# Delta-rule attention with two feed-forward layers on one core: triangles inverted in two halves joined on TensorE, two output products held over a group's end, square root by Newton steps

## The chip, the cores and the metric

One NeuronCore of a Trainium2 chip runs the whole program. TensorE does the matrix products (PE in the profile, its weight loads PEld), VectorE (DVE) and ScalarE (ACT) the elementwise work and the emptying of PSUM, GpSimd (POOL) some elementwise work between tiles of SBUF, and SyncE (SP) issues the DMAs. The metric is the device time of one execution in microseconds; lower is better.

## The reference

```python
B, H, S, D = 4, 8, 768, 48
k_n = k / (np.linalg.norm(k, axis=-1, keepdims=True) + 1e-06)
for t in range(S):                     # one 48x48 state for each of 4 x 8 heads
    y[:, :, t] = q_t @ state
    v_old = state.T @ k_t
    state = state + beta_t * outer(k_t, v_t - v_old)
x = y.transpose(0, 2, 1, 3).reshape(3072, 384)
x = (silu(x @ w_gate) * (x @ w_val)) @ w_out       # d_ff 1536
h = x @ w_in                                       # d_ff 2048
out = where(h > 0, h, exp(min(h, 0)) - 1) @ w_out2
```

## The kernel before, in words

**Groups.** The 3072 tokens are worked in 12 groups of 256: 128 steps of time of 2 of the 4 batches. A group holds 16 units (batch, head) of 128 time steps, and each unit is cut into 4 chunks of 32 steps, one on each 32 partitions. Within a chunk the recurrence is solved in closed form, which needs the inverse of a 32x32 unit triangular matrix: 64 triangles for a group.

**Attention of a group.** `norm` sums the squares of the keys (on GpSimd, into the buffer `ain`), takes the root on ScalarE (L168) and makes the factor 1/(norm + 1e-6) in six small instructions on VectorE (L170 to L175); `nkn` scales the keys (L184), `kb` multiplies by beta, `trans` transposes queries and keys on TensorE (L200), `gram` makes the 32x32 products of keys and of queries with keys (L210), and VectorE masks them into `gr` (L213). `inversion` brings the 64 triangles with `transpose` into a layout in which each partition holds half the columns of a triangle (L227) and solves them in SBUF on VectorE: for each row l from 31 down to 1 a product (L248, `mul`) and a sum (L255, `add`), over 16 - l//2 columns. Where such a step has over `CUT` = 40 elements it is made as two instructions, so that a group has 58 of each kind. `back` transposes the result (L263), and ScalarE copies it in four `spread` steps (L270) into `zt`, where the triangles of two chunks lie as a block diagonal of 64x64. `xstep` multiplies `R` (keys and values) by it with 32 products of 64x64 tiles (L281; the trace counts two instructions for each product of plain 32-bit floats, 64 here). Then come `gstep` (L294; ScalarE and VectorE take its results out of PSUM, L298 and L299), `chain` (the state from chunk to chunk, L312 and L316), `yall` (the outputs, L325), and `xtr` (outputs transposed and split in a high and a low part, `xh` and `xl`).

**First layer.** For each group and each of 12 blocks f of the hidden layer, `gv1` makes gate and value (18 products of 128x128 by 256 columns, L445) in one of two PSUM buffers `gv`. The result goes through ScalarE (Silu, L466), VectorE (L467), ScalarE (high part, L345) and VectorE (low part, L348) into one of `NHB` = 3 buffers `hb`. `out1` (9 products, L479) adds block f to `acc`, always two blocks behind `gv1` (`LAG` = 2); at the end of a group both that are left are made (`while held:` in `moe1`), then ScalarE copies `acc` out (L486) and it is stored to the buffer `x2d` in memory.

**Order.** `attention(g + 1)` and `moe1(g)` are lists of steps with weights, and `merge` sorts both together by the share of the weights that lies ahead of a step. The inversion of group g + 2 stands in the list of attention of group g + 1, its last fifth at the start of the next group (`XTR` = 0.8). From this order Tile sets each engine's own, and may move an instruction ahead where its inputs come early. Each engine works its queue strictly in order.

**Start and end.** Group 0 and the inversion of group 1 run while weights arrive and are decoded (64-bit words to floats, L389 to L409 and L345, L348, temporaries in turn). The second layer begins after group 11: `h2` (L514), the nonlinearity (L518 to L521), `out2` (L531); its weights are decoded through the temporaries `gr`, `st`, `zt`, `dt`.

Of the kernel before, what the change touches and what calls it, by code (L numbers as in the profile page):

```python
# [21 lines left out]
def delta_moe_kernel(ctx: ExitStack, tc: tile.TileContext, q, k, v, beta,  # L22
# [39 lines left out]
    NHB = 3  # L62
# [4 lines left out]
    zd = T("zd", [128, 2, 16])  # L67
# [8 lines left out]
    zt = T("zt", [128, 16, 64])  # L76
    st = T("st", [128, B, DM])
    sv = T("sv", [128, 2, C - 1, DM])
    sm = [T(f"sm{n}", [128, 16]) for n in range(5)]
# [25 lines left out]
    def emit_consts():  # L105
# [8 lines left out]
        fl = sm[0][:, 0:1]  # L114
        V.tensor_reduce(out=fl, in_=ident.rearrange("p (r h m) -> p h r m", r=4, h=2)[:, 1],
                        op=ALU.add, axis=AX.XY)

        V.tensor_copy(zd[:, 1, :], fl.to_broadcast([128, 16]))
        V.tensor_scalar(out=zd[:, 0, :], in0=zd[:, 1, :], scalar1=-1.0, scalar2=1.0,
                        op0=ALU.mult, op1=ALU.add)  # L120

    def emit_zero():
        V.memset(kp[:, :, D:64], 0.0)
        V.memset(qp[:, :, D:64], 0.0)
        G.memset(zt, 0.0)
# [36 lines left out]
    def norm(g):  # L162
        i, b0 = ax_of(g)
        sq = ain[:, 0:768].rearrange("p (u d) -> p u d", d=D)
        ss, s, r, t, w = sm
        (G if g > 0 else V).tensor_tensor(out=sq, in0=kp[:, :, 0:D], in1=kp[:, :, 0:D], op=ALU.mult)
        V.tensor_reduce(out=ss, in_=sq, op=ALU.add, axis=AX.X)
        A.activation(out=s, in_=ss, func=ACTF.Sqrt)  # L168

        V.tensor_scalar(out=r, in0=s, scalar1=1e-18, scalar2=None, op0=ALU.max)  # L170
        V.reciprocal(out=r, in_=r)
        V.tensor_tensor(out=t, in0=ss, in1=r, op=ALU.mult)
        V.tensor_tensor(out=t, in0=t, in1=s, op=ALU.add)
        V.tensor_scalar(out=t, in0=t, scalar1=-0.5, scalar2=-1e-6, op0=ALU.mult, op1=ALU.add)
        V.reciprocal(out=w, in_=t)  # L175
# [5 lines left out]
    def nkn(g, a):  # L181
        u = slice(a * 8, a * 8 + 8)
        kk = kp[:, u, 0:D]
        V.tensor_tensor(out=kk, in0=kk, in1=sm[4][:, u].unsqueeze(2).to_broadcast([128, 8, D]),  # L184
                        op=ALU.mult)
        A.copy(out=R[:, u, 0:D], in_=kk)
# [32 lines left out]
    def inversion():  # L219
        lst = []  # L220
        an = ain.rearrange("p (l j) -> p l j", l=32)

        def start(n):
            def f():
# [3 lines left out]
                if n == 0:  # L228
                    z = buf['z'] = TT("z", [128, 32, 16])
                    G.memset(z, 0.0)  # L230
                    V.tensor_copy(win(z[:, 0:1, 0:1], [[16, 2], [33, 16]]), zd)
# [3 lines left out]
        def step(l):  # L235
            c0 = l // 2
            cuts = [(c0, 16)]
            if l * (16 - c0) > CUT:
                cuts = [(c0, c0 + (16 - c0) // 2), (c0 + (16 - c0) // 2, 16)]

            b = 32 * (l + 1) % 1024
            ts = [ain[:, b + l * (x - c0):b + l * (y - c0)].rearrange("p (j n) -> p j n", n=y - x)
                  for x, y in cuts]

            def mul():
                z = buf['z']
                for (x, y), t in zip(cuts, ts):
                    V.tensor_tensor(out=t, in0=z[:, l:l + 1, x:y].to_broadcast([128, l, y - x]),  # L248
                                    in1=an[:, l, 0:l].unsqueeze(2).to_broadcast([128, l, y - x]),
                                    op=ALU.mult)  # L250

            def add():
                z = buf['z']
                for (x, y), t in zip(cuts, ts):
                    V.tensor_tensor(out=z[:, 0:l, x:y], in0=z[:, 0:l, x:y], in1=t, op=ALU.add)  # L255
            return [mul, add]
        for l in range(31, 0, -1):
            lst += step(l)

        def back():  # L260
            z = buf['z']
            t = ain[:, 0:512]
            V.transpose(out=t.rearrange("p (u i two) -> p i two u", u=16, two=2),  # L263
                        in_=z.rearrange("p a i -> p i a"))
        lst.append(back)

        def spread(r):
            def f():
                q0 = slice(32 * r, 32 * r + 32)
                A.copy(out=zt[q0, :, 32 * (r % 2):32 * (r % 2) + 32],  # L270
                       in_=ain[q0, 0:512].rearrange("p (u i) -> p u i", u=16))
            return f
        return lst + [spread(r) for r in range(4)]


    def xstep():
        for n in range(4):
            p = nxt(atb, "at")[:, 0:384].rearrange("p (n w) -> p n w", n=4)
            for j in range(4):
                for r in (0, 64):  # L280
# [507 lines left out]
```

## Time and profile before

| | |
|---|---|
| median of 3 runs | 1311.82 us (1307.21 to 1316.99) |
| span of the profiled execution, first to last instruction | 1301.1 us |
| median less that span: what lies around it | 10.7 us |
| TensorE busy, mean granted clock | 1162.0 us (89%), 0.949 |
| VectorE, ScalarE, GpSimd busy | 821.8, 608.6, 129.9 us |

The own time of the profiled execution is not among the three, only its span is known, so a change in the span is set against the median. Matmuls overlap in TensorE's pipeline: the time that a block of them takes is the step from its start to the start of the next block, not the sum of their durations. The granted clock is 1.00 at 2.4 GHz and 0.50 at 1.2 GHz; a stretch with a figure between holds some of both.

### The profile page before, as it was taken

How to read it: one execution, taken by the hardware profiler on the slowest of the kernel's cores; microseconds unless marked ns; L12 is line 12 of the kernel's file. 1: busy time of each engine (PE TensorE's matmuls, PEld its weight loads, DVE VectorE, ACT ScalarE, POOL GpSimd, SP SyncE). 2: the span in 40 equal slices, each digit the busy share in tenths (PEclk: the TensorE clock that was granted, in tenths of full speed). 3: DMA queues.
4: the chain of work that ended last, by engine and by line, in shares of the span. 5: the costliest groups of instructions: out<-in, count | busy, mean ns of one | idle time of the engine just before them, and what ended most of it. 6: DMA issues, size and time to landing. Idle time of an engine off the chain costs nothing.

```text
span 1301.1 us, 31342 instructions
## 1 busy us (share of the span) xinstructions
PE 1162.0 (89%) x13086; PEld 1078.5 (83%) x13086; DVE 821.8 (63%) x2709; ACT 608.6 (47%) x1181; POOL 129.9 (10%) x106
## 2 busy tenths in 40 slices
PE   2473999898989898989898989989899999999998
PEld 1363889898888898989888989978689899899897
DVE  6799585848484858585848574467964545454443
ACT  7554534343425252535353524457754545454443
POOL 4353100000000000000000000031300000000000
PEclk9866798889999999999999999989999999999999
DMA  9530202020202020202020100373010101000000
GB/s 298 160 81 1 38 14 39 13 39 10 43 2 51 2 50 2 51 2 50 7 46 2 26 11 5 125 251 104 1 49 1 49 1 49 1 33 1 25 1 25
DMA packets 106815, 57.16 MB, mean 44 GB/s; under 512 B 76945, under 2 KB 101521, under 8 KB 106673
## 3 DMA queue, kind: packets, MB, share of 16 engines
q1 hardware_dynamic: 106672, 55.16, 16.7%
q8 instruction: 102, 1.67, 0.5%
q14 instruction: 41, 0.33, 0.1%
HBM read 45.71 MB, written 9.44 MB: 42 GB/s over the span
## 4 chain that ended last, share of the span: by engine, by line
PE 57%; DVE 34%; ACT 4%; issue 3%; DMA 1%; POOL 1%; SPq 0%; DVEq 0%; ACTq 0%; POOLq 0%
PE gv L445 14%; DVE z L255 7%; DVE ain L248 7%; PE acc L531 7%; PE at L531 7%; PE at L514 7%; PE gv L514 7%; PE acc L479 5%; PE at L294 4%; DVE w L404 2%; PE at L281 2%; DVE hb L348 2%; DVE tb L467 2%; DVE ain L227 2%; PE at L312 2%
## 5 line engine op out<-in xcount | busy, mean ns | idle before, releaser
L445 PE MATMUL gv<-xh,w 128*128 128x256 f32 x1728 | 295.9, 295 | 23.6 <-DVE tb L467 22.9
L445 PEld LDWEIGHTS gv<-xh,w 128*128 128x128 f32 x1728 | 248.9, 200 | 29.4 <-DVE tb L467 24.0
L479 PE MATMUL acc<-hb,w 128*128 128x256 f32 x1296 | 194.9, 298 | 37.6 <-ACT hb L345 34.7
L479 PEld LDWEIGHTS acc<-hb,w 128*128 128x128 f32 x1296 | 172.2, 199 | 45.5 <-ACT hb L345 36.7
L445 PE MATMUL gv<-xl,w 128*128 128x256 f32 x864 | 160.6, 295 | 1.5 <-DVE xl L348 1.5
L466 ACT ACTIVATE tb<-gv 128x256 f32<-128x256 f32 x144 | 54.9, 382 | 216.4 <-PE gv L445 216.0
L467 DVE TENSOR_TENSOR tb<-gv,tb 128x256 f32<-128x256 f32 x144 | 60.7, 422 | 127.6 <-ACT tb L466 126.7
L445 PEld LDWEIGHTS gv<-xl,w 128*128 128x128 f32 x864 | 131.7, 202 | 2.9 <-DVE xl L348 1.7
L345 ACT CAST hb<-tb 128x256 fp32r<-128x256 f32 x144 | 58.4, 406 | 146.8 <-DVE tb L467 146.2
L255 DVE TENSOR_TENSOR z<-z,ain 128x60 f32<-128x60 f32 (+32 forms) x696 | 122.5, 214 | 1.3
L248 DVE TENSOR_TENSOR ain<-z,ain 128x60 f32<-128x60 f32 (+32 forms) x696 | 122.3, 207 | 1.2
L348 DVE TENSOR_TENSOR hb<-tb,hb 128x256 fp32r<-128x256 f32 x144 | 76.7, 533 | 42.7 <-ACT hb L345 41.3
L521 DVE SCALAR_TENSOR_TENSOR hb<-at,hb 128x512 f32<-128x512 f32 x48 | 33.2, 691 | 84.5 <-ACT hb L520 84.5
L521 DVE SCALAR_TENSOR_TENSOR hb<-gv,hb 128x512 f32<-128x512 f32 x48 | 33.1, 690 | 80.2 <-ACT hb L520 72.5
L294 PE MATMUL at<-gr,R 32*96 32x80 f32 x1536 | 75.3, 276 | 8.7 <-DVE w L299 4.4
L294 PEld LDWEIGHTS at<-gr,R 32*96 32x96 f32 x1536 | 64.9, 179 | 19.0 <-DVE w L299 4.6
L520 ACT ACTIVATE hb<-hb,neg 128x512 f32<-128x512 f32 x96 | 69.4, 723 | 2.8
L518 ACT ACTIVATE hb<-at 128x512 f32<-128x512 f32 x48 | 28.6, 595 | 87.6 <-PE at L514 87.6
L518 ACT ACTIVATE hb<-gv 128x512 f32<-128x512 f32 x48 | 28.6, 596 | 85.3 <-PE gv L514 85.0
L281 PE MATMUL at<-R,zt 64*64 64x96 f32 x768 | 38.6, 254 | 27.5 <-ACT zt L270 27.4
L519 ACT ACTIVATE hb<-hb 128x512 f32<-128x512 f32 x96 | 60.6, 632 | 2.7
L281 PEld LDWEIGHTS at<-R,zt 64*64 64x64 f32 x768 | 35.8, 140 | 29.7 <-ACT zt L270 28.2
(174 smaller groups left out, 2154.6 us busy)
## 6 DMA issues: line engine op xcount, KB each, us to landing
w<-in_moe_w_out_dram SPq DMA_DIRECT2D x28, 384.0 KB, 6.6
w<-in_moe_w_in_dram SPq DMA_DIRECT2D x16, 384.0 KB, 5.6
kp<-in_k_dram SPq DMA_DIRECT2D x12, 384.0 KB, 5.4
qp<-in_q_dram SPq DMA_DIRECT2D x12, 384.0 KB, 4.3
w<-in_moe_w_gate_dram SPq DMA_DIRECT2D x12, 384.0 KB, 7.8
w<-in_moe_w_val_dram SPq DMA_DIRECT2D x12, 384.0 KB, 8.0
R<-in_v_dram SPq DMA_DIRECT2D x24, 192.0 KB, 2.6
x2d<-hb SPq DMA_DIRECT2D x12, 256.0 KB, 2.1
```

Of the source, the lines that this page charges most:

```text
L248: V.tensor_tensor(out=t, in0=z[:, l:l + 1, x:y].to_broadcast([128, l, y - x]), in1=an[:, l, 0:l].unsqueeze(2).to_broadcast([128, l, y - x] ...
L255: V.tensor_tensor(out=z[:, 0:l, x:y], in0=z[:, 0:l, x:y], in1=t, op=ALU.add)
L281: nc.tensor.matmul(p[r:r + 64, j], lhsT=zt[r:r + 64, 4 * n + j, :], rhs=R[r:r + 64, 4 * n + j, :], start=True, stop=True, skip_group_check ...
L294: nc.tensor.matmul(ps_[c][0:96, s * 80:s * 80 + 80], lhsT=R[t, u, :], rhs=gr[t, u, 0:80], start=True, stop=True, skip_group_check=True)
L348: (e2 or V).tensor_tensor(out=lo, in0=src, in1=hi.bitcast(F32), op=ALU.subtract)
L445: nc.tensor.matmul(dst, lhsT=wt[:, a_, kk * 128:(kk + 1) * 128], rhs=xx[:, kk, :], start=(n == 0), stop=(n == 3 * KD - 1))
L467: V.tensor_tensor(out=s, in0=p[:, TB:2 * TB], in1=s, op=ALU.mult)
L479: nc.tensor.matmul(o, lhsT=w[:, a_, d * 128:(d + 1) * 128], rhs=hh[:, b_, :], start=(f == 0 and n == 0 and d != 1), stop=(f == F1 - 1 and ...
L514: nc.tensor.matmul(p, lhsT=W[f][:, 0, a_, kk * 128:(kk + 1) * 128], rhs=x2[n][b_][:, kk, :], start=(m == 0), stop=(m == 3 * KD - 1))
L520: A.activation(out=r, in_=r, func=ACTF.Identity, bias=neg1, scale=1.0)
L521: V.scalar_tensor_tensor(out=r, in0=p, scalar=0.0, in1=r, op0=ALU.max, op1=ALU.add)
L531: nc.tensor.matmul(ob4[t], lhsT=hh[:, b_, t * 128:(t + 1) * 128], rhs=w[:, a_, :], start=(f == 0 and m == 0), stop=(f == F2 - 1 and m == 2))
```

## The change

**Inversion.** A triangle is cut into two diagonal blocks of 16x16 and the block below them. VectorE inverts both diagonal blocks in the same instructions, 15 rows instead of 31, and no step is cut in two: 15 products and 15 sums for a group. `back` makes a second transpose, of the whole buffer. `join1` multiplies the block-diagonal inverse by the triangle on TensorE (64 products with 16 rows, 32x32 tiles into one PSUM bank), VectorE adds the unit diagonal and masks (one instruction over 128x512 from PSUM), `join2` multiplies once more on TensorE (64 products), and one copy of 128x512 on ScalarE fills `zt`, in place of the four `spread` copies. `xstep` then has 64 products of 32x32 tiles in place of 32 of 64x64.

**Held products.** Two blocks of `out1` are left over at a group's end and made in the next group; `NHB` is 4.

**Root.** ScalarE's square root and the six instructions are replaced by 13 on VectorE: a first guess from the bits, three Newton steps of three instructions, two more and a reciprocal. `zt` is half as large and no temporary of the decoding any more (`t2`).

```diff
-    NHB = 3
+    NHB = 4
...
-    zd = T("zd", [128, 2, 16])
+    zd = T("zd", [128, 2])
...
-    zt = T("zt", [128, 16, 64])
+    zt = T("zt", [128, 16, 32])
+    eye = T("eye", [128, 32])
+    low = zd[:, 1:2]
...
-        ss, s, r, t, w = sm
+        ss, s, r = sm
         (G if g > 0 else V).tensor_tensor(out=sq, in0=kp[:, :, 0:D], in1=kp[:, :, 0:D], op=ALU.mult)
         V.tensor_reduce(out=ss, in_=sq, op=ALU.add, axis=AX.X)
-        A.activation(out=s, in_=ss, func=ACTF.Sqrt)
-
-        V.tensor_scalar(out=r, in0=s, scalar1=1e-18, scalar2=None, op0=ALU.max)
-        V.reciprocal(out=r, in_=r)
-        V.tensor_tensor(out=t, in0=ss, in1=r, op=ALU.mult)
-        V.tensor_tensor(out=t, in0=t, in1=s, op=ALU.add)
-        V.tensor_scalar(out=t, in0=t, scalar1=-0.5, scalar2=-1e-6, op0=ALU.mult, op1=ALU.add)
-        V.reciprocal(out=w, in_=t)
+        V.tensor_scalar(out=s.bitcast(I32), in0=ss.bitcast(I32), scalar1=-0.5,
+                        scalar2=float(0x5f3759df), op0=ALU.mult, op1=ALU.add)
+        for _ in range(3):
+            V.scalar_tensor_tensor(out=r, in0=s, scalar=-0.5, in1=ss, op0=ALU.mult, op1=ALU.mult)
+            V.tensor_tensor(out=r, in0=r, in1=s, op=ALU.mult)
+            V.scalar_tensor_tensor(out=s, in0=r, scalar=1.5, in1=s, op0=ALU.add, op1=ALU.mult)
+        V.tensor_tensor(out=r, in0=ss, in1=s, op=ALU.mult)
+        V.tensor_scalar(out=r, in0=r, scalar1=-1.0, scalar2=-1e-6, op0=ALU.mult, op1=ALU.add)
+        V.reciprocal(out=s, in_=r)
...
+        d1 = ain[:, 0:512].rearrange("p (u j) -> p u j", u=16)
+        d1t = ain[:, 512:1024].rearrange("p (u j) -> p u j", u=16)
...
         def step(l):
             c0 = l // 2
-            cuts = [(c0, 16)]
-            if l * (16 - c0) > CUT:
-                cuts = [(c0, c0 + (16 - c0) // 2), (c0 + (16 - c0) // 2, 16)]
-
-            b = 32 * (l + 1) % 1024
-            ts = [ain[:, b + l * (x - c0):b + l * (y - c0)].rearrange("p (j n) -> p j n", n=y - x)
-                  for x, y in cuts]
+            n = 8 - c0
+            t = win(ain[:, 512:513], [[8, 2], [32, l], [1, n]])
 
             def mul():
                 z = buf['z']
-                for (x, y), t in zip(cuts, ts):
-                    V.tensor_tensor(out=t, in0=z[:, l:l + 1, x:y].to_broadcast([128, l, y - x]),
-                                    in1=an[:, l, 0:l].unsqueeze(2).to_broadcast([128, l, y - x]),
-                                    op=ALU.mult)
+                V.tensor_tensor(out=t, in0=win(z[:, l:l + 1, c0:c0 + 1], [[264, 2], [0, l], [1, n]]),
+                                in1=win(ain[:, 32 * l:32 * l + 1], [[528, 2], [1, l], [0, n]]),
+                                op=ALU.mult)
 
             def add():
-                z = buf['z']
-                for (x, y), t in zip(cuts, ts):
-                    V.tensor_tensor(out=z[:, 0:l, x:y], in0=z[:, 0:l, x:y], in1=t, op=ALU.add)
+                z = win(buf['z'][:, 0:1, c0:c0 + 1], [[264, 2], [16, l], [1, n]])
+                V.tensor_tensor(out=z, in0=z, in1=t, op=ALU.add)
             return [mul, add]
-        for l in range(31, 0, -1):
+        for l in range(15, 0, -1):
             lst += step(l)
 
         def back():
-            z = buf['z']
-            t = ain[:, 0:512]
-            V.transpose(out=t.rearrange("p (u i two) -> p i two u", u=16, two=2),
-                        in_=z.rearrange("p a i -> p i a"))
-        lst.append(back)
-
-        def spread(r):
-            def f():
-                q0 = slice(32 * r, 32 * r + 32)
-                A.copy(out=zt[q0, :, 32 * (r % 2):32 * (r % 2) + 32],
-                       in_=ain[q0, 0:512].rearrange("p (u i) -> p u i", u=16))
-            return f
-        return lst + [spread(r) for r in range(4)]
+            V.transpose(out=ain[:, 0:512].rearrange("p (u i two) -> p i two u", u=16, two=2),
+                        in_=buf['z'].rearrange("p a i -> p i a"))
+            V.transpose(out=d1t, in_=d1)
+
+        def join1():
+            p = buf['jp'] = nxt(atb, "at").rearrange("p (u j) -> p u j", u=16)
+            for u in range(16):
+                for c in range(C):
+                    r = 32 * c
+                    nc.tensor.matmul(p[r:r + 32, u],
+                                     lhsT=gr[r:r + 16, u, 80:112],
+                                     rhs=d1t[r:r + 16, u], start=True, stop=True,
+                                     skip_group_check=True)
+            v = buf['v'] = TT("z", [128, 16, 32])
+            V.scalar_tensor_tensor(out=v, in0=p, scalar=low[:, 0:1],
+                                   in1=eye.unsqueeze(1).to_broadcast([128, 16, 32]),
+                                   op0=ALU.mult, op1=ALU.add)
+
+        def join2():
+            p = nxt(atb, "at").rearrange("p (u j) -> p u j", u=16)
+            for u in range(16):
+                for c in range(C):
+                    t = slice(32 * c, 32 * c + 32)
+                    nc.tensor.matmul(p[t, u], lhsT=buf['v'][t, u], rhs=d1[t, u], start=True,
+                                     stop=True, skip_group_check=True)
+            A.copy(out=zt, in_=p)
+        return lst + [back, join1, join2]
...
     def xstep():
         for n in range(4):
             p = nxt(atb, "at")[:, 0:384].rearrange("p (n w) -> p n w", n=4)
             for j in range(4):
-                for r in (0, 64):
-                    nc.tensor.matmul(p[r:r + 64, j], lhsT=zt[r:r + 64, 4 * n + j, :],
-                                     rhs=R[r:r + 64, 4 * n + j, :], start=True, stop=True,
+                for c in range(C):
+                    t = slice(32 * c, 32 * c + 32)
+                    nc.tensor.matmul(p[t, j], lhsT=zt[t, 4 * n + j, :],
+                                     rhs=R[t, 4 * n + j, :], start=True, stop=True,
                                      skip_group_check=True)
             A.copy(out=R[:, 4 * n:4 * n + 4, :], in_=p)
...
-        while held:
+        while held and g == NB - 1:
             put(1, held.pop(0), 1.0, out1)
...
-        t2 = ("gr", "st", "zt", "dt")
+        t2 = ("gr", "st", "dt")
```

On TensorE, at the end of a group, the order was this (`w14` and `w17` are the pairs that hold `out1`'s weights, `hb1` and `hb2` with the numbers 280 and 282 belong to the last two blocks, `w0` is the first `gv1` of the next group):

```order
L479 MATMUL acc_85<-hb0_278_7430,w14_53_926 128x256 x9
L479 MATMUL acc_85<-hb1_280_7487,w17_60_1086 128x256 x9
L445 MATMUL gv0_83<-xh1_268_7172,w0_21_203 128x256
L479 MATMUL acc_85<-hb2_282_7542,w17_60_1086 128x256 x9
L445 MATMUL gv0_83<-xh1_268_7172,w0_21_203 128x256 x2
L445 MATMUL gv0_83<-xl1_269_7173,w0_21_203 128x256 x3
```

And this is what stands there now, from the end of the next group's first `gv1` on:

```order
L460 MATMUL gv0_82<-xh1_274_7795,w0_21_210 128x256 x3
L270 MATMUL at1_86<-ain_72,gr_71 32x32 x64
L494 MATMUL acc_84<-hb2_288_8081,w17_61_1096 128x256 x8
L284 MATMUL at2_87<-ain_72,z_293_8221 32x32 x64
L494 MATMUL acc_84<-hb2_288_8081,w17_61_1096 128x256
L460 MATMUL gv1_83<-xh1_274_7795,w1_22_229 128x256 x3
L460 MATMUL gv1_83<-xl1_275_7796,w1_22_229 128x256 x2
L296 MATMUL at3_88<-R_69,zt_73 32x96 x16
L296 MATMUL at0_85<-R_69,zt_73 32x96 x16
L296 MATMUL at1_86<-R_69,zt_73 32x96 x16
```

Before, both products of the end stood in a row with only one instruction between them; now the first gv1 of the next group and `join1` stand ahead of the eleventh block's product, and `join2`, the second gv1, `xstep` and the first `gstep` ahead of the twelfth's.

On ScalarE at the same place, the queue was (`zt<-ain` are the spread copies, `tb1_281` and `hb2_282` the last block's):

```order
L345 CAST hb1_280_7487<-tb0_279_7484 128x256
L270 COPY zt_73<-ain_72 32x16x32 x2
L466 ACTIVATE tb1_281_7539<-gv1_84 128x256
L270 COPY zt_73<-ain_72 32x16x32 x2
L345 CAST hb2_282_7542<-tb1_281_7539 128x256
L486 COPY hb0_283_7572<-acc_85 128x512
L486 COPY hb1_284_7575<-acc_85 128x256
```

Now it is (`tb1_289` and `hb3_290` are the last block's, `tb0_291` and `hb0_292` the next group's first):

```order
L360 CAST hb2_288_8081<-tb0_287_8078 128x256
L481 ACTIVATE tb1_289_8111<-gv1_83 128x256
L360 CAST hb3_290_8114<-tb1_289_8111 128x256
L481 ACTIVATE tb0_291_8148<-gv0_82 128x256
L360 CAST hb0_292_8151<-tb0_291_8148 128x256
L286 COPY zt_73<-at2_87 128x512
L299 COPY R_69<-at3_88 128x384
L299 COPY R_69<-at0_85 128x384
```

The copies into `zt` stood ahead of the last block's Silu and cast; the one copy now stands behind them and behind those of the next group's first block.

On TensorE in group 0, whose queue ran into `xstep` so (`w5` with `hb2` is the third block's product):

```order
L479 MATMUL acc_85<-hb2_66_1152,w5_33_522 128x256 x9
L445 MATMUL gv1_84<-xh0_39_681,w7_35_605 128x256 x3
L445 MATMUL gv1_84<-xl0_40_682,w7_35_605 128x256
L281 MATMUL at1_87<-R_69,zt_73 64x96
L281 MATMUL at2_88<-R_69,zt_73 64x96
L281 MATMUL at3_89<-R_69,zt_73 64x96
L281 MATMUL at0_86<-R_69,zt_73 64x96
```

it now runs:

```order
L460 MATMUL gv1_83<-xh0_40_762,w7_36_686 128x256 x3
L494 MATMUL acc_84<-hb3_70_1430,w5_34_603 128x256 x3
L270 MATMUL at3_88<-ain_72,gr_71 32x32 x64
L494 MATMUL acc_84<-hb3_70_1430,w5_34_603 128x256 x6
L460 MATMUL gv0_82<-xh0_40_762,w9_39_759 128x256 x2
L284 MATMUL at0_85<-ain_72,z_62_1166 32x32 x64
L460 MATMUL gv0_82<-xh0_40_762,w9_39_759 128x256
L460 MATMUL gv0_82<-xl0_41_763,w9_39_759 128x256 x3
L460 MATMUL gv0_82<-xh0_40_762,w9_39_759 128x256 x2
L296 MATMUL at1_86<-R_69,zt_73 32x96 x16
```

The fourth `gv1` and its product now stand whole ahead of `xstep`, and part of the fifth.

## Rows read from the trace of the kernel before

**Rows 1.** The profile page: busy time, share of the span and instructions of each engine.

```profile
PE 1162.0 (89%) x13086; PEld 1078.5 (83%) x13086; DVE 821.8 (63%) x2709; ACT 608.6 (47%) x1181; POOL 129.9 (10%) x106
```

**Rows 2.** The chain of waits of the whole span, one piece: the xstep of group 2.

```profile
192.92 2.79 PE at L281 x64
```

**Rows 3.** The chain of waits in 776 to 906 us, pieces.

```profile
785.38 2.79 PE at L281 x64
...
795.52 2.35 PE gv L445 x18
...
814.01 2.16 PE gv L445 x18
816.17 1.50 PE at L325 x128
```

**Rows 4.** Stretches of a group: length, busy time by engine, granted clock, DMA, GB/s.

```profile
588.70:653.50 64.80, 60.16 (x925) 56.93 (x924) 44.06 (x195) 26.63 (x63) 4.70 (x5) 0.97 0.15 26
...
642.20:646.30 4.10, 0.01 (x1) 0.00 (x0) 1.06 (x3) 3.25 (x6) 1.44 (x2) 1.00 0.00 0
646.30:648.40 2.10, 2.06 (x9) 1.76 (x10) 2.10 (x2) 0.00 (x0) 1.07 (x1) 0.59 0.00 0
648.40:653.50 5.10, 5.10 (x39) 4.97 (x38) 2.24 (x10) 4.03 (x6) 0.00 (x0) 0.83 0.24 80
```

**Rows 5.** PE's instructions in order of time: start, us, line, count, [idle before].

```profile
46.87 6.34 PE L281 MATMUL at<-R,zt 64*64 64x96 f32 x64 [26.95 <-ACT zt L270]
...
127.75 1.01 PE L445 MATMUL gv<-xh,w 128*128 128x256 f32 x3 [11.56 <-DVE tb L467]
...
646.31 2.40 PE L479 MATMUL acc<-hb,w 128*128 128x256 f32 x9 [4.09 <-ACT hb L345]
...
791.52 0.92 PE L294 MATMUL at<-gr,R 32*96 32x80 f32 x32
...
853.88 0.96 PE L514 MATMUL at<-lc,w 128*128 128x512 f32 x3 [2.16 <-ACT w L345]
```

**Rows 6.** ACT's instructions in order of time, at the end of that group.

```profile
642.91 1.25 ACT L270 COPY zt<-ain 32x512 f32<-32x512 f32 x2 [2.41 <-DVE ain L263]
644.18 0.38 ACT L466 ACTIVATE tb<-gv 128x256 f32<-128x256 f32 x1
...
645.85 0.40 ACT L345 CAST hb<-tb 128x256 fp32r<-128x256 f32 x1
```

**Rows 7.** DVE's instructions in order of time: the inversion, then the end of that group.

```profile
619.18 0.19 DVE L248 TENSOR_TENSOR ain<-z,ain 128x31 f32<-128x31 f32 x1
619.41 0.21 DVE L255 TENSOR_TENSOR z<-z,ain 128x31 f32<-128x31 f32 x1
...
641.75 1.07 DVE L263 STREAM_TRANSPOSE ain<-z 128x512 f32<-128x512 f32 x1
...
646.29 1.36 DVE L348 TENSOR_TENSOR hb<-tb,hb 128x256 fp32r<-128x256 f32 x1 [1.26 <-ACT hb L345]
...
651.16 0.17 DVE L170 TENSOR_SCALAR sm<-sm 128x16 f32<-128x16 f32 x1 [2.65 <-ACT sm L168]
```

**Rows 8.** The chain of waits in 588 to 656 us, by line, then pieces.

```profile
by line: PE gv L445 22.5%; DVE z L255 11.2%; DVE ain L248 11.0%; PE at L281 7.7%; PE acc L479 6.9%; PE at L294 6.5%; DVE hb L348 4.3%; DVE tb L467 4.0%; DVE ain L227 3.2%; ACT zt L270 2.8%; PE at L312 2.6%; PE at L200 2.6%; issue 2.3%; DVE 
...
602.22 0.39 ACT tb L466
...
603.53 0.80 DVE hb L348
...
607.98 1.75 PE at L200 x16
```

**Rows 9.** DVE in order of time, second layer: one instruction over 128x512 from PSUM.

```profile
887.20 0.69 DVE L521 SCALAR_TENSOR_TENSOR hb<-gv,hb 128x512 f32<-128x512 f32 x1 [7.71 <-PE at L514]
```

**Rows 10.** All engines in order of time, the squares on POOL.

```profile
645.90 1.47 POOL L166 TENSOR_TENSOR ain<-kp 128x768 f32<-128x768 f32 x1 [1.89 <-ACT zt L270]
```

**Rows 11.** A stretch after group 3's xstep, columns as in rows 4.

```profile
269.60:276.40 6.80, 6.70 (x59) 6.16 (x62) 2.25 (x8) 3.35 (x10) 0.83 (x1) 0.62 0.16 31
```

More of the change, by code (lines that the diff above doesn't have):

```diff
@@ L75, in delta_moe_kernel @@
     ain = T("ain", [128, 1024])
-    zt = T("zt", [128, 16, 64])
+    zt = T("zt", [128, 16, 32])
+    eye = T("eye", [128, 32])
+    low = zd[:, 1:2]
     st = T("st", [128, B, DM])
     sv = T("sv", [128, 2, C - 1, DM])
-    sm = [T(f"sm{n}", [128, 16]) for n in range(5)]
+    sm = [T(f"sm{n}", [128, 16]) for n in range(3)]
     neg1 = T("neg1", [128, 1])
@@ L112, in emit_consts @@
                             pattern=[[1, 32]], channel_multiplier=-1)
-        fl = sm[0][:, 0:1]
-        V.tensor_reduce(out=fl, in_=ident.rearrange("p (r h m) -> p h r m", r=4, h=2)[:, 1],
+        for r in range(4):
+            q0 = slice(32 * r, 32 * r + 32)
+            V.tensor_copy(eye[q0], ident[q0, q0])
+        V.tensor_reduce(out=low, in_=ident.rearrange("p (r h m) -> p h r m", r=4, h=2)[:, 1],
                         op=ALU.add, axis=AX.XY)
-        V.tensor_copy(zd[:, 1, :], fl.to_broadcast([128, 16]))
-        V.tensor_scalar(out=zd[:, 0, :], in0=zd[:, 1, :], scalar1=-1.0, scalar2=1.0,
+        V.tensor_scalar(out=zd[:, 0:1], in0=low, scalar1=-1.0, scalar2=1.0,
                         op0=ALU.mult, op1=ALU.add)
@@ L124, in emit_zero @@
         V.memset(qp[:, :, D:64], 0.0)
-        G.memset(zt, 0.0)
         G.memset(st[0:32], 0.0)
@@ L183, in nkn @@
         kk = kp[:, u, 0:D]
-        V.tensor_tensor(out=kk, in0=kk, in1=sm[4][:, u].unsqueeze(2).to_broadcast([128, 8, D]),
+        V.tensor_tensor(out=kk, in0=kk, in1=sm[1][:, u].unsqueeze(2).to_broadcast([128, 8, D]),
                         op=ALU.mult)
@@ L230, in f @@
                     G.memset(z, 0.0)
-                    V.tensor_copy(win(z[:, 0:1, 0:1], [[16, 2], [33, 16]]), zd)
+                    V.tensor_copy(win(z[:, 0:1, 0:1], [[16, 2], [33, 16]]),
+                                  zd.unsqueeze(2).to_broadcast([128, 2, 16]))
             return f
@@ L632, in delta_moe_kernel @@
     POOL = 0
-    CUT = 40
     LAG = 2
```

## The prediction

> **What bounds the kernel now.** I read the page first, then the chain of waits of one steady group, then TensorE (PE) in order of time where a group ends, with the stretches there. The page puts PE at 89% of the span, DVE at 63% and ACT at 47% [rows 1]: PE is the bound, and the question is where its other 11% lies. The `xstep` of group 2 (counted from 0) starts at 192.92 [rows 2] and that of group 11 at 785.38 [rows 3]: nine intervals of a group in 592.5 us, 65.8 on average, where a steady one takes 64.80 [rows 4]. What is left is a start, in which PE waits 26.95 us for `zt` and once 11.56 us for DVE's `tb` [rows 5], and an end after group 11.
>
> Within a steady group PE stands still in one place of 4.10 us, at the group's end [rows 4], and the idle time is put down to ACT's `hb` [rows 5]. The other group ends look alike. PE's wait names a cast on ACT, but ACT's own rows show what made that late: ACT waited 2.41 us for the transpose of the inversion, copied `zt` at 642.91 and only then came to the last block's Silu (644.18) and cast (645.85) [rows 6]. The transpose began at 641.75 and took 1.07 [rows 7]. So DVE's inversion ends last, and PE pays for it through ACT's queue. The chain of waits agrees: the sums and products of the inversion (L255, L248) are 22.2% of its 68 us [rows 8], 15.1 us, which end in front of that cast.
>
> The stop costs more than its own length. After it the granted clock is 0.59 for 2.10 us and 0.83 for 5.10 us [rows 4]: 2.1 × 0.41 + 5.1 × 0.17 = 1.7 us lost. Without stop and slow clock this group would take 64.8 − 4.1 − 1.7 = **59.0 us**, the floor that I add to.
>
> **The inversion.** Removed on DVE: 58 products and 58 sums; added, 15 and 15. A dependent pair steps by 619.41 − 619.18 = 0.23 us [rows 7], so some 15.1 us of chain become 30 × 0.23 = 6.9, plus a second transpose (1.07, the first's duration) and one instruction from PSUM, for which I take 0.69, a row of the same size from PSUM [rows 9]. DVE then needs 8.7 where it needed 15.1, the transposes are through 5 to 6 us before the group's end, and the wait of 4.1 goes, with its slow clock. That DVE has room again is worth nothing more by itself: PE is next, everywhere else in the group.
>
> Added on PE: two times 64 products, 128 instructions each, in 32x32 tiles. The trace has no such tile. Nearest is `yall` (L325), 128 instructions in 1.50 us [rows 3], 12 ns each; `xstep`, in 64x64 tiles with 96 columns, has 64 in 2.79 us [rows 3], 44 ns each. `trans` gives the price of a column where nothing overlaps: 16 instructions of 128 columns in 1.75 us [rows 8], 0.85 ns a column. So `xstep`'s 64 × 96 columns would be 5.2 us one after the other, and in 2.79 two tiles nearly overlap. With four tiles at a time 128 × 32 columns are 128 × 32 × 0.85 / 4 = 0.9 us, by `yall` 1.5. I take 1.35 for each join (bounds 1.0 and 1.5, leaving a start of the pipeline), nearer to `yall`, since both are many small products: **+2.7**. They stand between products of full size; a `gv1` that is entered from other work stepped 2.35, an undisturbed one 2.16 [rows 3], so each join brings a switch of 0.2: **+0.4**.
>
> `join2` waits for DVE's instruction, and what is queued behind it on PE is the last product of the eleventh block, the second `gv1` and `xstep`. In front of DVE's instruction stands the low part of the next group's first block: Silu to the end of the low part is 602.22 to 603.53 + 0.42, about 1.75 [rows 8] (0.80 in the row is with its waiting), and with 0.69 that is 2.5 us from the end of the first `gv1`. PE has `join1` (1.35) and eight of nine products (0.96) until then, 2.3. I charge **+0.25** (0 to 1; DVE's row at 646.29 took 1.36 beside POOL's work [rows 7, 10]).
>
> The copy into `zt` is one of 128x512 on ACT, some 0.6 us from half of the row of two at 642.91 [rows 6]; in front of `xstep` PE has one product and five of `gv1`, 0.7 us. Nothing, but it has no margin. `xstep` itself has twice the products with half the rows: in four tiles at a time the same 96 columns take the same **2.8** (case C below says otherwise).
>
> **The held products.** No work is added: 18 products move from before the boundary behind it. What they buy is that PE has `gv1` and `join1` to do while the last two blocks go through ACT and DVE, so the chain ACT-DVE-ACT-DVE of the last block no longer ends in front of PE. ACT's queue has the Silu and cast ahead of the copy now, which removes the 4.1 a second time: either part alone might do that. `NHB` = 4 pays for the longer life of `hb`. `acc` is finished later, behind `xstep`, and its copy and store have a group of time.
>
> **The root.** ACT loses a root and the change of table around it, and DVE's wait of 2.65 us for it goes [rows 7]. In its place stand 13 small instructions, at the inversion's step of 0.23 some 3.0 us, where six took 1.4. This lies behind the boundary, in front of DVE's emptying of `gstep` (L314). POOL's squares (1.47 [rows 10]) must wait for `join2`, which reads the same buffer, so `norm` starts a little later than before. The wait of 2.65 and the 13 instructions about cancel; for `gstep` and `chain` coming late I charge **+0.5** (0 to 1.0).
>
> **The clock.** The steady group loses nothing besides the 1.7 above, but the mean interval is 1.0 longer than the steady one, and one place where it goes is 269.60 to 276.40, after the `xstep` of group 3: 6.8 us at 0.62 with PE busy for 6.70 [rows 11], between pieces of `gstep`; 6.8 × 0.38 = 2.6 us. So the clock also falls with no stop ahead of it. The change puts 256 more small instructions there. I charge a loss of **0.85** a group, one such stretch in every third group (0 to 3.4: one in each group, and 0.8 of lesser ones).
>
> The sum of a group: 59.0 + 2.7 + 0.4 + 0.25 + 0.5 + 0.85 = 63.7, against the mean of 65.8: 2.1 less, times nine intervals, **−19 us**.
>
> **Start and end.** In group 0 PE waits for `zt` until 46.87 [rows 5]; the inversion of group 0 is shorter by 6 us, but ACT and the decoding stand in its way, so I take −3 for it. The inversion of group 1 lies in a stretch that DVE bounds (the wait of 11.56 for `tb` at 127.75 [rows 5]): −2 of its 6; and one more `gv1` and `out1` stand ahead of group 0's `xstep` and fill waiting time, 2.2 + 1.3, −3. Together **−8** (0 to −14). At the end `zt` is no temporary of the decoding any more, and the last two products of group 11 remain; PE waited 2.16 there for a decoded weight [rows 5]. I take **−2** (−5 to +3).
>
> Together −29: the span goes from 1301.1 to 1272. The profiled execution's own time isn't known, but the median lies 10.7 above its span; set against the median, 1311.8 − 29 = **1282**.
>
> **Rivals.** B: *the clock falls in every group*, as at 269.60, since `join1`, `join2`, `xstep` and `gstep` now come within some 10 us. Then a group loses 3.4 and not 0.85, 2.55 × 9 = +23: 1305. For it: that stretch lies beside small tiles. Against: the steady group has the same tiles, and its only loss follows a stop.
>
> C: *only two small tiles overlap*, as two do in `xstep` now. Then `xstep` takes 64 × 2 × 96 × 0.85 / 2 = 5.2 in place of 2.8 (+2.4), and each join 1.75 (+0.8 for both): 3.2 × 12 groups = +38: 1320. `yall`, with 12 ns an instruction, speaks against it.
>
> D, the slow side: *products of different row strips into one PSUM bank run one at a time.* Then `xstep` takes 128 × 96 × 0.85 = 10.4 us and each join 3.5: 7.6 + 4.3 = +11.9 over my sum in each of 12 groups, +143: 1425. It decides from the point at which joins and `xstep` together take over 5.5 + 29 / 12 = 7.9 us. For it: `gstep`, whose 32 instructions of 80 columns in four strips took 0.92 [rows 5], 29 ns each and not 68, has a bank for each strip. Against it: two strips of 64 rows went into one bank in `xstep` at 44 ns, not 82 [rows 3]. The Trainium skill, "TensorEngine Tiling (Array Packing)", section "Restrictions and Gotchas", says that different row tiles cannot access the same PSUM bank simultaneously, which is case D; for two strips the trace disagrees (44 ns an instruction), for four no row here shows it.
>
> E, better: no clock loss, joins at 1.0 and no wait at `join2`: 59.0 + 2.0 + 0.4 + 0.25 = 61.65, 2.05 × 9 = −18 more, and the start at its best, −7: 1257.
>
> That nothing happens at all is part of B and C: DVE's chain off the path, and its worth spent on PE.
>
> **Chances.** The forecast 1282 with its own bounds, 1262 to 1298: 0.58; E 0.15; B 0.14; C 0.08; D 0.05. The range takes in E and B, 1256 to 1306. Within 1% is 1298.7 to 1324.9, about what a measurement of this kernel can tell from no change. B and C, less the part of B under that line and with the upper edge of the forecast, give 0.15 there; D and the upper tail of C 0.07; the rest, 0.78, is faster.
>
> **What would show it.** PE without idle time over 1 us at the group ends, and granted clock 1.00 there; DVE's L263 transposes ended before the last block's Silu; the two joins at 1.35 each and `xstep` at 2.8 (over 5 is C, over 10 is D); idle time of PE ahead of `join2` under 0.5; intervals between `xstep` near 63.7; the first `xstep` near 44. The prediction is wrong if the new wait at `join2` or at `chain` is over 2 us, or a stretch under 0.7 of clock stands in each group.

## The result and the profile after

The changed kernel takes **1269.69 us** (median of 4 runs, 1266.85 to 1271.71) against 1309.51 for the kernel before (4 runs, 1300.85 to 1316.99): ratio **0.970, 95% interval 0.965 to 0.976**. The profiled span is 1269.8 us, 31.3 under the 1301.1 of before. The experiments show where it comes from: the held products, with their fourth buffer and without the joined inversion, give more than the whole change, and the joined inversion, once the products are held, costs time.

First the page of the changed kernel (engines, then the DMA queue that carries instructions).

```profile
PE 1178.4 (93%) x16926; PEld 1089.8 (86%) x16926; DVE 733.0 (58%) x1788; ACT 561.9 (44%) x1112; POOL 127.0 (10%) x105
...
q8 instruction: 132, 2.16, 0.7%
```

VectorE is down by 89 us [rows 1] and PE up by 16. `xstep` starts in group 2 at 181.15 and in group 11 at 748.95 (before: 192.85 and 785.31 by PE's own first instruction, 0.07 ahead of the pieces in [rows 2] and [rows 3]), so nine intervals take 567.8 us, 63.1 each. The nine intervals before and after, then two of those of the changed kernel (columns as in [rows 4]):

```profile
192.85:785.31 592.46, 548.97 (x8317) 521.36 (x8317) 396.18 (x1740) 241.21 (x570) 40.69 (x44) 0.96 0.14 25
181.15:748.95 567.80, 553.37 (x11201) 522.25 (x11200) 332.64 (x1045) 203.84 (x515) 41.21 (x45) 1.00 0.12 26
...
368.80:433.50 64.70, 61.69 (x1244) 57.98 (x1243) 37.09 (x116) 22.71 (x57) 4.67 (x6) 1.00 0.12 27
433.50:495.50 62.00, 61.10 (x1243) 57.68 (x1242) 36.83 (x116) 22.59 (x57) 4.65 (x6) 1.00 0.12 28
```

PE's idle time in the nine intervals falls from 43.5 us to 14.4, and its busy time rises by only 4.4, although the joins add more. The granted clock is 1.00 in every interval from group 2 on; before, it was 0.96 over the nine. That difference is worth some 24 us (an estimate, 0.04 of 592.46). PE in order of time at a group's end:

```profile
551.97 1.29 PE L270 MATMUL at<-ain,gr 16*32 16x32 f32 x128
553.18 1.21 PE L494 MATMUL acc<-hb,w 128*128 128x256 f32 x8
554.59 0.45 PE L284 MATMUL at<-ain,z 32*32 32x32 f32 x30 [0.19 <-DVE z L275]
555.63 1.03 PE L284 MATMUL at<-ain,z 32*32 32x32 f32 x98 [0.59 <-issue]
556.58 0.38 PE L494 MATMUL acc<-hb,w 128*128 128x256 f32 x1
556.81 0.52 PE L460 MATMUL gv<-xh,w 128*128 128x256 f32 x3
557.16 0.40 PE L460 MATMUL gv<-xl,w 128*128 128x256 f32 x2
557.49 0.70 PE L296 MATMUL at<-R,zt 32*32 32x96 f32 x24
559.48 2.35 PE L296 MATMUL at<-R,zt 32*32 32x96 f32 x104 [1.29 <-issue]
```

The stop of 4.09 at [rows 5] is gone. `join1` takes 1.29 us, `join2` waits 0.19 for VectorE, and then comes something that no step of mine had: PE stands still 0.59 us in the middle of `join2` and 1.29 in the middle of `xstep`, waiting for nothing that the profile shows. PE's waits over the whole span, summed (us in total, times, longest):

```profile
PE at L284 <- issue: 9.0, 10, 3.3
PE at L296 <- issue: 5.3, 7, 1.3
...
PE at L284 <- DVE z L275: 2.4, 9, 0.9
...
PE acc L494 <- ACT hb L501: 1.6, 1, 1.6
```

### The profile page after: what moved, and what is told of

Read it like the earlier page. It is cut to its first block, busy times and chain, and to the rows that moved or that the text cites. A ratio compares the mean times of both kernels' runs of the same rounds, so it can differ in the third digit from the quotient of the medians.

```text
span 1269.8 us, 38044 instructions
## 1 busy us (share of the span) xinstructions
PE 1178.4 (93%) x16926; PEld 1089.8 (86%) x16926; DVE 733.0 (58%) x1788; ACT 561.9 (44%) x1112; POOL 127.0 (10%) x105
## 3 DMA queue, kind: packets, MB, share of 16 engines
q8 instruction: 132, 2.16, 0.7%
## 4 chain that ended last, share of the span: by engine, by line
PE 73%; DVE 15%; issue 8%; ACT 2%; DMA 1%; POOL 0%; SPq 0%; DVEq 0%; POOLq 0%; ACTq 0%
PE gv L460 19%; PE acc L494 10%; PE gv L529 7%; PE acc L546 7%; PE at L546 7%; PE at L529 7%; PE at L309 5%; PE at L327 3%; PE at L296 2%; DVE w L419 2%; PE at L204 2%; DVE z L255 2%; PE at L214 1%; DVE ain L249 1%; PE at L340 1%
## 5 line engine op out<-in xcount | busy, mean ns | idle before, releaser
L460 PE MATMUL gv<-xh,w 128*128 128x256 f32 x1728 | 289.4, 290 | 11.0 <-DVE tb L482 9.6
L460 PEld LDWEIGHTS gv<-xh,w 128*128 128x128 f32 x1728 | 241.3, 194 | 15.8 <-DVE tb L482 10.2
L494 PEld LDWEIGHTS acc<-hb,w 128*128 128x128 f32 x1296 | 167.4, 193 | 7.8 <-DVE hb L363 1.9
L460 PE MATMUL gv<-xl,w 128*128 128x256 f32 x864 | 155.6, 288 | 0.2 <-issue 0.2
L360 ACT CAST hb<-tb 128x256 fp32r<-128x256 f32 x144 | 58.4, 406 | 112.4 <-DVE tb L482 111.2
L363 DVE TENSOR_TENSOR hb<-tb,hb 128x256 fp32r<-128x256 f32 x144 | 66.4, 461 | 41.5 <-ACT hb L360 41.5
L309 PEld LDWEIGHTS at<-gr,R 32*96 32x96 f32 x1536 | 60.4, 174 | 19.2 <-issue 3.6
L169 POOL TENSOR_TENSOR ain<-kp 128x768 f32<-128x768 f32 x11 | 16.1, 1467 | 305.0 <-PE at L284 305.0
L255 DVE TENSOR_TENSOR z<-z,ain 128x30 f32<-128x30 f32 (+4 forms) x180 | 42.9, 238 | 5.0
L296 PE MATMUL at<-R,zt 32*32 32x96 f32 x1536 | 39.8, 252 | 6.1 <-issue 5.3
L529 PE MATMUL gv<-lc,w 128*128 128x512 f32 x144 | 41.9, 400 | 2.9 <-DVE hb L536 2.9
```

What stands on the lines that cost most here:

```text
L255: V.tensor_tensor(out=z, in0=z, in1=t, op=ALU.add)
L296: nc.tensor.matmul(p[t, j], lhsT=zt[t, 4 * n + j, :], rhs=R[t, 4 * n + j, :], start=True, stop=True, skip_group_check=True)
L309: nc.tensor.matmul(ps_[c][0:96, s * 80:s * 80 + 80], lhsT=R[t, u, :], rhs=gr[t, u, 0:80], start=True, stop=True, skip_group_check=True)
L363: (e2 or V).tensor_tensor(out=lo, in0=src, in1=hi.bitcast(F32), op=ALU.subtract)
L460: nc.tensor.matmul(dst, lhsT=wt[:, a_, kk * 128:(kk + 1) * 128], rhs=xx[:, kk, :], start=(n == 0), stop=(n == 3 * KD - 1))
L494: nc.tensor.matmul(o, lhsT=w[:, a_, d * 128:(d + 1) * 128], rhs=hh[:, b_, :], start=(f == 0 and n == 0 and d != 1), stop=(f == F1 - 1 and ...
```

## The experiments

Every median stands beside the kernel before on the same chip (1301 to 1306 us), and the ratio is to that. Differences between two changed kernels are given between their medians, which come from different chips; by the ratios they come out up to 6 us otherwise.

**Tiles.** `x32` changes `xstep`'s tiles alone, with what hangs on them (`zt`, the temporaries).

```diff
-    zt = T("zt", [128, 16, 64])
+    zt = T("zt", [128, 16, 32])
...
-                for r in (0, 64):
+                for c in range(C):
+                    t = slice(32 * c, 32 * c + 32)
...
-        t2 = ("gr", "st", "zt", "dt")
+        t2 = ("gr", "st", "dt")
```

> The kernel before with only xstep in 32x32 tiles (zt half as wide, the four copies kept, three temporaries of the decoding instead of four). Theory: four tiles at a time cost the same 2.8 us, the group ends stay as they were, and the end of the program loses some 5 us by the missing temporary: 1309 to 1317 us. Rival (twice the instructions cost a stop of PE of some 0.6 us in each group, as after join2 in the changed kernel): 7 us more, 1318 to 1325. Rival (tiles of four row strips take turns): over 1400.

1301.94 us, ratio 0.998 (0.995 to 1.001): no difference. PE's wait at the group's end is untouched (34.7 us in ten waits before):

```profile
PE acc L479 <- ACT hb L345: 33.5, 10, 4.1
```

Behind group 11's `xstep` 514.5 us follow, against 515.8 before: the missing temporary costs nothing, where I had expected 5.

**The hold on top of it.** `x32_held`, against `x32`:

```diff
-    NHB = 3
+    NHB = 4
...
-        while held:
+        while held and g == NB - 1:
```

> The same with the two last output products of a group held into the next (NHB 4). The inversion keeps its 58 steps and still ends late on VectorE, and its copies stand ahead of a cast of the held blocks on ScalarE. Theory: PE gets one gv1 of 2.2 us into the stop of 4.1, so about half of it goes, with part of the low clock behind it: 2 to 4 us a group, 1275 to 1295 us. Rival (either part of the change alone takes the whole stop): 1265 to 1275. Rival (the stop only moves ahead of xstep, which waits for zt): 1308 to 1318, as x32.

**1247.46 us, ratio 0.957 (0.951 to 0.962)**: better than all that I expected, and 22 us better than the whole change (18 by the ratios). A steady interval, and then all engines in order of time at a group's end:

```profile
485.88:544.32 58.44, 58.44 (x988) 55.55 (x987) 42.73 (x194) 26.24 (x63) 4.71 (x6) 1.00 0.17 29
```

```profile
597.87 1.16 DVE L262 STREAM_TRANSPOSE ain<-z 128x512 f32<-128x512 f32 x1
...
599.11 0.62 ACT L269 COPY zt<-ain 32x512 f32<-32x512 f32 x1 [3.24 <-DVE ain L262]
599.64 0.40 ACT L345 CAST hb<-tb 128x256 fp32r<-128x256 f32 x1
600.06 1.90 ACT L269 COPY zt<-ain 32x512 f32<-32x512 f32 x3
...
602.75 0.45 PE L281 MATMUL at<-R,zt 32*32 32x96 f32 x12
```

PE is busy 58.44 of 58.44 us at full clock; the mean of the nine intervals is 59.3. The inversion still ends last, at 599, where the next group begins, and `zt` still waits for it; but PE now has the next group's first `gv1` (599.33) and the eleventh block's product (601.58) to do, and `xstep` starts at 602.75 without a wait.

**Inversion alone, and the root.** `inv_only` is the changed kernel with the products released (`NHB` = 3) and the old root; `inv_held` puts back the root only.

```diff
-        while held and g == NB - 1:
+        while held:
```

```diff
+        A.activation(out=s, in_=ss, func=ACTF.Sqrt)
-        for _ in range(3):
...
+        V.tensor_scalar(out=r, in0=s, scalar1=1e-18, scalar2=None, op0=ALU.max)
```

> The changed kernel with the products released at the group's end as before (NHB 3) and with the old root: the inversion in two halves alone. Theory: ScalarE is no longer held by the inversion, PE waits 0.5 to 1 us for the last block's chain (Silu to low part 1.75 us against one product of 1.2), and the joins cost 2.6: about 1280 to 1290 us. Rival (holding the products is what removes the stop): 1305 to 1315. Rival (either part does all): 1266 to 1274.

> The changed kernel with ScalarE's square root and the six instructions put back. Theory: the root is beside the path, its wait of 2.65 us and the 13 Newton instructions about cancel: within 5 us of the changed kernel, 1268 to 1275 us. Rival (VectorE's emptying of gstep waits for the norm, so each us of it counts): 1 to 3 us a group, 1280 to 1300.

`inv_only` 1279.87 us, ratio 0.981 (0.976 to 0.986); `inv_held` 1277.95, ratio 0.979 (0.974 to 0.985). The ten waits for `hb` at the groups' ends are gone in both, so the short inversion too removes the stop by itself (the 0.5 to 1 us of wait that I expected of `inv_only` there is not seen), and the hold on top of it adds nothing to tell from zero. The rival of `inv_held` was nearer: the root costs some 8 us here (12 by the ratios). The groups of `inv_held` show why, in all engines in order of time:

```profile
572.27 0.17 DVE L173 TENSOR_SCALAR sm<-sm 128x16 f32<-128x16 f32 x1 [2.21 <-ACT sm L171]
...
576.36 0.70 PE L308 MATMUL at<-gr,R 32*96 32x80 f32 x6 [0.35 <-DVE lc L313]
577.30 0.40 PE L308 MATMUL at<-gr,R 32*96 32x80 f32 x4 [0.24 <-DVE lc L313]
```

The norm begins only when `join2` has read `ain`, so with 2.21 us of waiting in it VectorE empties `gstep` late, and PE waits 0.59; the clock falls behind it in five of the nine intervals (at 579.18 in this one, to 0.50 for 3.41 us). In `inv_only` the same two short waits stand at 580 and 581, behind a stop of 0.76 us in `xstep`, and there too the clock falls. PE in order of time, then two stretches:

```profile
572.09 2.83 PE L295 MATMUL at<-R,zt 32*32 32x96 f32 x125 [0.76 <-issue]
...
580.07 0.70 PE L308 MATMUL at<-gr,R 32*96 32x80 f32 x6 [0.35 <-DVE lc L313]
581.01 1.21 PE L308 MATMUL at<-gr,R 32*96 32x80 f32 x26 [0.24 <-DVE lc L313]
...
571.00:580.00 9.00, 7.88 (x188) 6.89 (x187) 4.30 (x13) 6.26 (x13) 1.25 (x2) 1.00 0.01 4
580.00:590.00 10.00, 9.59 (x114) 8.70 (x114) 3.87 (x14) 4.91 (x15) 0.83 (x1) 0.66 0.11 21
```

A clock of 0.66 over 10 us holds more of 1.2 than of 2.4 GHz and costs 3.4 us; the clock falls in six of the nine intervals of `inv_only`.

**One product held.** `x32_held1`, against `x32_held`:

```diff
-        while held and g == NB - 1:
+        while len(held) > (1 if g < NB - 1 else 0):
```

> As the run with hold, 32x32 tiles and NHB 4 and the long inversion, but only the last product is held over a group's end. Theory: it is the twelfth block's product that stops PE, and what the hold gives is cover, one gv1 of 2.2 us ahead of xstep where two held products give 3.4; the copies into zt then end some 1 us behind it: 0.5 to 1.5 us a group more than with both held, 1252 to 1262 us. Rival (the eleventh block's product waits as well): 2 us or more a group, 1266 to 1300. Rival (one held product is as good as two): 1244 to 1250.

1272.99 us, ratio 0.975 (0.970 to 0.979): a steady group takes 61.4, 3.0 more than with two. The theory was wrong, and so is the reason of the rival whose range holds the time: PE does the eleventh block's product at 617.10 without a wait. ScalarE's order is another again, and then one line of PE:

```profile
620.68 1.25 ACT L269 COPY zt<-ain 32x512 f32<-32x512 f32 x2 [2.25 <-DVE ain L262]
621.95 0.38 ACT L466 ACTIVATE tb<-gv 128x256 f32<-128x256 f32 x1
622.36 1.25 ACT L269 COPY zt<-ain 32x512 f32<-32x512 f32 x2
623.64 0.41 ACT L345 CAST hb<-tb 128x256 fp32r<-128x256 f32 x1
...
629.24 0.47 ACT L284 COPY R<-at 128x384 f32<-128x384 f32 x1
...
622.85 0.62 PE L445 MATMUL gv<-xh,w 128*128 128x256 f32 x3 [0.87 <-DVE tb L467]
```

The Silu of the last block stands behind two copies, so PE waits 0.87 us for a `gv` buffer at 622.85, and `xstep`'s results, copied behind two more Silus, hold up `gstep` by 0.78: 1.65 of the 3.0. A wait of 0.5 for `gstep`'s own results makes it 2.2; the rest isn't accounted for. With two held, the last block's Silu stands even behind all four copies (601.99), and nothing waits for it: the `gv1` that needs its buffer comes only behind `xstep`, at 605.52, where with one held it stands ahead of it, at 622.85. So the second held product gives more than cover: `xstep` no longer stands behind that `gv1`.

**The buffer and the root without joins.** `held3` is the kernel before with nothing but the line of the hold (`NHB` = 3); `x32_held_root` is `x32_held` with the Newton steps of the change.

> The kernel before with the hold alone, one line: xstep in 64x64 tiles, four copies, the long inversion, ScalarE's root and NHB 3 all as before. Theory: the hold is what counts and the fourth buffer is not: within 5 us of the run with hold, 32x32 tiles and NHB 4 (1247), so 1242 to 1253. Rival (the fourth buffer is needed, the copies of acc and the casts of the next blocks wait for one another): 1 to 3 us a group more, 1257 to 1285.

> Hold, 32x32 tiles in xstep and NHB 4 with the long inversion, and the Newton steps in place of the root. Theory: the root is worth something only where the joins push the norm back; here no product of PE waits behind it in the steady groups: within 3 us of 1247. Rival (the root is on the path everywhere, 8 us as in the changed kernel): 1236 to 1241.

`held3` 1259.91 us, ratio 0.966 (0.963 to 0.969): one line is as good as the whole change, and 12 us are missing against `x32_held`, which has the fourth buffer and the 32x32 tiles besides (the tiles alone gave nothing in `x32`). It waits for `gstep`'s results in eight places, and the clock is 0.97 in six of nine intervals; whether that is the buffer or the order around it is open.

```profile
PE at L294 <- DVE dt L299: 6.9, 8, 1.6
```

`x32_held_root` 1246.60, ratio 0.957 (0.954 to 0.959): the root is worth nothing where nothing waits behind it.

**What stops PE inside a run of products.** In the changed kernel the idle times without a cause lie a whole number of 128 products apart. Stretches from one to the next:

```profile
555.62:559.48 3.86, 2.56 (x128) 2.17 (x128) 1.17 (x3) 0.59 (x1) 2.47 (x2) 1.00 0.03 6
559.48:618.98 59.50, 58.79 (x1150) 55.74 (x1151) 35.75 (x114) 22.00 (x56) 2.19 (x3) 1.00 0.13 29
618.98:622.55 3.57, 3.08 (x127) 2.69 (x128) 1.17 (x3) 1.07 (x2) 2.47 (x2) 1.00 0.02 5
```

128 products and 128 weight loads are 256 instructions of PE; 1150 and 1151 are nine times 256, less 3. The queue for instructions moved 132 packets of 2.16 / 132 = 16.4 KB, and PE's 2 × 16926 instructions are 132.2 times 256. In the kernel before 2 × 13086 are 102.2 times 256, and its page has

```profile
q8 instruction: 102, 1.67, 0.5%
```

So the theory is that PE's instructions arrive in blocks of 256, and that a block of small products is used up before the next is there. Two kernels, each the changed one with the same 64 products more in each inversion, beside `join2` or in its middle, separate that from mere work:

```diff
+        def spare():
+            p = nxt(atb, "at").rearrange("p (u j) -> p u j", u=16)
...
+                    nc.tensor.matmul(p[t, u], lhsT=gr[t, u, 80:112], rhs=gr[t, u, 80:112],
+                                     start=True, stop=True, skip_group_check=True)
...
+            spare()
```

> The changed kernel with 64 more products of 32x32 tiles in each inversion (of masked keys with themselves, never read), issued beside join2, so that three such runs and xstep follow closely. Theory (PE runs out of loaded instructions in a dense run of small products): 1.3 us of their own and one more stop of 0.6 to 1.0 us in each of 11 groups: 21 to 26 us more than the changed kernel, 1290 to 1296. Rival (only their own time counts): 14 to 17 us more, 1283 to 1287.

> The changed kernel with the same 64 products more in each inversion, but issued in the middle of the inversion, between blocks of full-size products. Theory: 1.3 us of their own and 0.2 of a switch, and no more stops than in the changed kernel: 15 to 18 us more, 1284 to 1288, some 6 us or more under the dense one. Rival (a stop comes with every so many instructions wherever they stand): the same time as the dense one.

Apart: 1280.12 us, ratio 0.982 (0.981 to 0.984), 10 us more than the changed kernel (15 by the ratios, where I had expected 15 to 18). Dense: **1322.40, ratio 1.015 (1.014 to 1.017)**, 53 more, twice what I expected. PE in the dense run:

```profile
584.77 0.35 PE L247 MATMUL at<-gr 32*32 32x32 f32 x19 [2.00 <-issue]
...
588.52 0.48 PE L292 MATMUL at<-ain,z 32*32 32x32 f32 x19 [2.43 <-issue]
...
589.94 2.29 PE L503 MATMUL acc<-hb,w 128*128 128x256 f32 x9
```

Two stops of 2 us or more, 128 products and 3.75 us apart; the idle time without a cause is 43.6 us in 26 places, against 19.5 in 20 in `spare_apart` and 17.9 in 22 in the changed kernel, and the nine products behind take 2.29 in place of 1.2, at a clock of 0.50 (0.94 to 0.98 over each of the nine intervals). Instructions and work are the same in both kernels, so where they stand is what costs.

The packets' own times settle the theory. In the changed kernel packets of PE's queue came from 553.00 to 554.14 and from 556.75 to 558.14, and PE went on at 555.63 and 559.48. In all thirteen traces, the kernel before included, there are 150 such stops over 0.15 us. Each of them ends 193 or 194 instructions past a multiple of 256 in the count of PE's instructions, 1.2 to 1.6 us after a packet has ended, and behind a block of 256 in which at most 18 of some 128 products are full-size ones of the two layers.

**Joins far from `xstep`.** `xtr1`:

```diff
-    XTR = 0.8
+    XTR = 1.0
```

> The changed kernel with the whole inversion and both joins in the list of the group before (XTR 1.0), so that two gv1 and two to three products of out1 stand between join2 and xstep. Theory: the stops of PE inside join2 and xstep come from the dense run of small products, and mostly go when xstep is taken out of it: 14 us of such idle time become 5 to 8, 1259 to 1265 us. Rival (a stop comes in each join anyway, or elsewhere in the group): 1268 to 1273.

1269.22 us, ratio 0.971 (0.965 to 0.977): no gain, the rival holds. `xstep` has one stop of 0.2 us left, but those of `join2` grew from 9.0 to 11.7 us: the two joins are a run dense enough by themselves.

**The better part of each.** `mixed`, against the changed kernel, takes hold, `NHB` = 4, 32x32 tiles and Newton steps everywhere, and the joined inversion for groups 0 and 1 alone.

```diff
-        inv = inversion()
+        inv = inversion(nx < 2)
```

> Hold, NHB 4, 32x32 tiles and Newton steps everywhere; the inversion in two halves with its joins only for groups 0 and 1, whose chains VectorE bounds, and the long inversion with its four copies from group 2 on, where PE is the bound. Theory: the joins gain 9 us before group 2's xstep (181.2 against 190.2) and lose some 31 in the nine groups behind (63.1 us a group against 59.7), so this gets the one without the other: 1234 to 1241 us. Rival (the gain at the start is lost again, as group 2's inversion then runs into the longer work of the start): 1244 to 1249.

**1233.30 us (6 runs), ratio 0.946 (0.943 to 0.949)**, the fastest of all and just under what I expected: group 2's `xstep` starts at 176.97, against 190.19 in `x32_held_root`, and an interval takes 58.9 us (median of nine).

## Why the prediction came out right

Sign and range held, 1269.7 in 1256 to 1306, and the mean of the nine intervals came out at 63.1 where the sum said 63.7. That agreement owes something to errors which cancel.

**Read rightly: the stop, its chain and its price.** A steady group of `x32_held` has neither stop nor slow clock and takes 58.4 us; the floor worked out from 4.1 of stop and 1.7 of clock was 59.0.

**Failed: what removes it.** I wrote that the short inversion takes the wait away and that the held products remove "the 4.1 a second time: either part alone might do that", and then charged the joins in full as the price of the first. The medians in us (the old root, but for the last row) show that the half-sentence was the point:

| | released | held |
|---|---|---|
| long inversion, 32x32 tiles | 1301.9 | 1247.5 |
| joined inversion | 1279.9 | 1278.0 |
| long inversion, Newton steps | | 1246.6 |
| joined inversion, Newton steps | | 1269.7 |

Either part alone ends the stop; together they end it once and pay for the joins. The inversion that "ends last" did not have to be shorter: PE had to have some 3.4 us of other work in front of it (599.33 to 602.75 in `x32_held`).

**The terms.** Joins 2.7: measured 1.21 and 1.40 by PE's steps, the stop taken off, 2.6. Wait at `join2` 0.25: 0.19. Switches 0.4: not seen, since 128 instructions apart lengthen an interval by 1.1 us (64.2 against 63.1), less than the 1.2 that `join1` takes. `gstep` late 0.5: none in the steady groups with the Newton steps, 0.59 with the root, and the clock behind it. Clock 0.85: none in the changed kernel; rival B is what `inv_only` shows, in six of nine intervals. The stops for instructions were in no term and are the largest error: 12.5 us from group 2 to 11, 1.4 a group; by them my sign "PE without idle time over 1 us at the group ends" failed. They could have been found: the kernel before has five of them there, 5.3 us, none in the group of the floor. I looked for the 1.0 us by which the mean interval is longer than that group in the clock alone; 0.6 of it is these. So three terms that came to 1.75 and were not paid stand against one of 1.4 that was left out, and the agreement of 63.7 with 63.1 is in part luck. Cases C and D fell: `join1` takes 10 ns an instruction, where 32 columns one after the other would be 27, and `xstep`'s 128 take 2.8 us as before (602.75 to 605.52 in `x32_held`). So the Trainium skill's sentence on row tiles and one PSUM bank ("TensorEngine Tiling (Array Packing)", "Restrictions and Gotchas") does not hold for these products, whose four strips write different partitions of it.

**Start and end.** I gave −8 and −2; it was −11.7 and +5.1, the latter outside its bounds. PE's busy time behind the last `xstep` is 501.1 us where it was 496.8. One `gv1` more stands there (22 blocks, where there were 21), 2.2 us, and the clock is at 0.50 for 3.4 us more (824.48 to 831.30 and 858.61 to 862.02, before 854.89 to 861.72), which is 1.7. In the same way 13 products of `gv1` and 9 of `out1`, some 2.6 us, moved behind group 2's `xstep`. So 2 to 3 us of both numbers are work counted on the other side of a mark.

**The base.** I put the change in the span on the median. In the later runs of the kernel before 1.7 us lie around the span, not 10.7, and its time goes with the mean clock, from 1299.2 us at 0.954 to 1311.7 at 0.940: the profiled execution was a quick one of some 1303. That is 9 of the 13 us by which the median lies under my sum. The span fell by 31.3 where I had said 29; the medians are 39.8 apart. Two small slips in the sums change nothing: 1311.8 − 29 is 1283, and the best start of rival E is 6 us under my term, which gives 1258.

## What to carry to other kernels

A wait that ends on a slow chain can be removed by a shorter chain or by work put ahead of the waiting engine; try the second first, since it adds nothing, and never count the first as worth its wait when both are made. Make a part that buys time on one engine with work on another only in the stretch that the first engine bounds: the joins gain some 9 us before group 2 and lose some 31 behind it (181.15 against 190.19, and nine intervals of 63.1 against 59.7, the changed kernel beside `x32_held_root`). Before many small products are set in a row, count PE's instructions, not only their columns.

## What the runs showed of the hardware

PE's instructions come in blocks of 256, one packet of 16.4 KB each (132 packets for 33852 products and weight loads, 102 for 26172). PE's idle times without a cause all end at one place in that count, 1.2 to 1.6 us after a packet has ended. Where blocks hold products of 10 ns, as in `spare_dense`, the second stop of a pair ends 3.45 to 3.75 us after the first (ten pairs), though PE waits for nothing else: some 14 ns an instruction (an estimate, 3.6 us by 256). In none of the thirteen traces does such a stop follow a block made mainly of full-size products; the five of the kernel before follow blocks of `gram` and `yall`.

In `inv_only` a stop of 0.76 us in `xstep` and two waits of 0.35 and 0.24 us in `gstep` were followed by a clock of 0.66 over 10 us, while the changed kernel, with stops of 0.59 and 1.29 us in `join2` and `xstep` and no wait in `gstep`, kept 1.00: what decides between the two, these runs do not settle.
